# Tables of a state-space kernel laid out in groups of four columns

## The chip, the cores and the metric

One Trainium2 chip, one of its cores. The metric is the device time of one execution in microseconds (us); lower is better. A core has a matrix engine (PE, TensorE), a vector engine (DVE), a scalar engine (ACT), a general engine (POOL, GpSimd) and a queue engine (SP), each running its own instruction stream, held together by semaphores. Operands lie in SBUF, 128 partitions of some 200 KB; matmuls write to PSUM, 128 partitions with eight banks of 512 float32 values.

## What is computed

A layer of a state-space model with an MLP behind it, on a sequence of 2048 positions with 512 channels (all inputs bfloat16):

```python
def _A_ref(u, A_re, A_im, B_re, B_im, C_re, C_im, log_dt, Dskip):
    dt = jnp.exp(log_dt)[:, None]
    A = A_re + 1j * A_im; Bc = B_re + 1j * B_im; Cc = C_re + 1j * C_im
    logdA = dt * A
    dB = dt * Bc
    P = jnp.exp(logdA[:, :, None] * l[None, None, :])
    K = jnp.einsum("dn,dnl,dn->dl", Cc, P, dB).real
    # y = causal convolution of u with K (by FFT of length 4096), per channel
    return y + u * Dskip
def _B_ref(x, w1, b1, w2, b2):
    y = _layernorm(x)
    return _gelu(y @ w1 + b1) @ w2 + b2
h = x + _A_ref(_layernorm(x), ...)
return h + _B_ref(_layernorm(h), ...)
```

The part that matters here is K: for each of 512 channels d, a sum over n = 128 states of a complex exponential in the tap l. The kernel splits l into a coarse and a fine index, so that each channel's taps are a product of two small tables: 20 entries of the one kind (A) times 33 of the other (B), each with a real and an imaginary part.

## The kernel before

**Data.** All of SBUF is one arena `ar`; a view `V` is an offset, a type and a shape in it. The 512 channels are four blocks c = 0 to 3 of CW = 128 columns. For each block there are four tables, partition = state n: `EA[c]` and `IA[c]` (real and imaginary part, NA = 20 rows of 128 columns, bf16), `EB[c]` and `IB[c]` (NB = 33 rows). They are declared in L519 to L522, row by row: the element of row k and column d is at k*128 + d, so one column's entries are 256 bytes apart.

**How the tables are made.** The scalar engine writes magnitudes: `bexps` (L742 to L745) has 16 exponentials, each of which writes two rows (16 − e0 and 16 + e0) of all four blocks of EB, 1024 elements; `aexps` (L947 to L958) has 10, each for four rows of two blocks of EA. POOL sets the middle rows of EB and IB (L1360, L1361). Then come the angles. `chain` (L963 to L1011) does it for the B tables of two blocks at a time: matmuls (L979, L984) accumulate the angle in PSUM as an integer phase, the scalar engine takes 16 sines of 1024 elements (L992), and the vector engine multiplies magnitude by sine and cosine, the rows below the middle in reversed order and separately for real and imaginary part (L1004), the rows above in one instruction of 2048 elements for both (L1010). `chain1` (L1013 to L1035) does the same for the A table of one block: matmuls L1025 and L1028, 20 sines L1030, and 20 products L1034, each of which writes four rows of IA and EA by one instruction with two parts.

**How the taps are made.** `kgen` (L1042 to L1072), once for each block: for each of the 128 columns d two matmuls add into one PSUM area, L1058 with weights = column d of EA (128 x 20) and moving data = column d of EB (128 x 33), L1059 with IA and IB. Four column groups g of the array work at the same time, on columns 32g + i. Groups of 11, 11 and 10 values of i share a bank each (`KIS`); in a bank the sums lay as [k][i], k = 0 to 32: a matmul's 33 sums are n*4 bytes apart, n = 11 or 10. The work on the matrix engine comes in pieces of five or six i, and between the pieces the order puts other work. After it an eviction (L578 on the scalar, L580 on the vector engine) of 726 elements and one of 330 convert the sums to bf16 in `Kg` or `kgc`, whose innermost index is i; L1072 then adds the skip term.

**What stands around it.** `kspec` (L1074, matmuls L1088) and `kspec1` (L1100, matmuls L1113) take the taps to the spectrum; `lnorm` (L874, POOL's power at L649, L654, L882, L884) normalizes the input, `austage` (L897) and `fstage` (L918, L922) transform it; `inverse` (L1203, L1213) goes back, and the MLP (L1330, L1332, L1346, L1348) follows to the end.

**The order.** Nothing is scheduled on the chip. `S.add` records each operation with what it reads and writes; the list `ORDER` (L269 to L304) gives the order in which operations are written out, hence the order on each engine, and `SLOTS` the PSUM banks. An operation waits for an earlier one where the accesses of the two overlap.

Of the kernel before, what the change touches and what calls it, by code (L numbers as in the profile page):

```python
# [20 lines left out]
CW = 128  # L21
NCH = 4
# [221 lines left out]

class Two:
# [7 lines left out]
class VS(V):  # L253
# [57 lines left out]
class Sched:  # L311
    def __init__(self):
        self.ops = []
        self.wr, self.rd = {}, {}
        self.pr = 0.0

    def keys(self, x):
        if isinstance(x, V):
            return [(g, q) for q in range(x.p0 // 32, (x.p1 - 1) // 32 + 1) for g in range(x.lo // GK, (x.hi - 1) // GK + 1)]
        return (x,)  # L320

    def add(self, eng, cost, fn, r=(), w=(), new=(), lat=0.0, pr=None, byts=0, soft=(), softw=(), hv=None):
# [10 lines left out]
        for x in r:  # L333
            for k in self.keys(x):
                p = self.wr.get(k)
                if p is not None:
                    deps.add(p)
        for x in w:
            for k in self.keys(x):
# [67 lines left out]
def kernel(ctx, tc, A_u, A_A_re, A_A_im, A_B_re, A_B_im, A_C_re, A_C_im, A_log_dt, A_Dskip,  # L407
# [111 lines left out]
    EA = [at(EAo[c // 2] + c % 2 * ASZ, bf16, NA, CW) for c in range(NCH)]  # L519
    EB = [at(EB0 + c * BSZ, bf16, NB, CW) for c in range(NCH)]  # L520
    IA = [at(IAo[c // 2] + c % 2 * ASZ, bf16, NA, CW) for c in range(NCH)]
    IB = [at(IBo[c // 2] + c % 2 * BSZ, bf16, NB, CW) for c in range(NCH)]  # L522
# [219 lines left out]
    def bexps(pr):  # L742
        for e0 in range(1, 17):
            add("ACT", c_act(1024) + 0.03, lambda e, e0=e0: act.activation(multi(EB0, BSZ, bf16, NCH, NB, CW)[:, :, 16 - e0:17 + e0:2 * e0, :].rearrange("p c k d -> p k c d"), th.ap().rearrange("p k (c d) -> p k c d", c=NCH), ACT.Exp, scale=float(8 * e0)),  # L744
                r=[th, TBL], w=[EB[c][16 + z * e0] for z in (1, -1) for c in range(NCH)], pr=pr + 0.01 * e0)  # L745
# [183 lines left out]
    def ent(lo0, q, lo, n, rev=False):  # L929

        a = ar[:, lo0 // 2:lo0 // 2 + q].rearrange("p (c q) -> p c q", c=2)
        o = lo // 2
        a = a[:, :, o:o + n * CW].rearrange("p c (e d) -> p c e d", e=n)
        return a[:, :, ::-1, :] if rev else a

    def free(off, dims):

        a = ar[:, 0:1]
        return bass.AP(a.tensor, a.offset + off, [list(a.ap[0])] + dims)
# [4 lines left out]
    def regs(lo0, q, lo, n):  # L944
        return [at(lo0 + q * c + lo, bf16, n, CW) for c in range(2)]

    def aexps(hf, pr):  # L947
        for n in range(5):
            p = Ps()

            def fn(e, p=p, n=n):
                for j in range(4):
                    for g in range(4):
                        pe.matmul(pst(p)[32 * g:32 * g + 32, 256 * j:256 * j + 256], lhsT=W3[4 * n + j].ap(), rhs=S3[hf][g].ap(), start=True, stop=True, tile_position=(0, 32 * g))
            S.pr = pr + 0.01 * n
            add("PE", 0.45, fn, r=[W3, S3[hf]], w=[p], new=[p], soft=[TBL])
            add("ACT", c_act(1024), lambda e, p=p, n=n, hf=hf: act.activation(multi(EAo[hf] + 4 * n * 256, ASZ, bf16, 2, 4, CW).rearrange("p c a d -> p a c d"), pst(p).rearrange("p (a c d) -> p a c d", a=4, c=2), ACT.Exp),  # L957
                r=[p, TBL], w=[EA[2 * hf + c][4 * n + z] for c in range(2) for z in range(4)])  # L958
# [4 lines left out]
    def chain(hf, kind, pr):  # L963
# [4 lines left out]
        for gn, b0 in enumerate(groups):  # L968
# [3 lines left out]
            for cs in range(2):  # L972
# [19 lines left out]
                add("ACT", c_act(1024), lambda e, p=p, sc=sc, cs=cs: act.activation(sc[cs].ap().rearrange("p c e d -> p e c d"), pst(p, i16).rearrange("p (e c d two) -> p e c d two", e=4, c=2, two=2)[:, :, :, :, 0], ACT.Sin, scale=SINSC), r=[p, TBL], w=[sc[cs]])  # L992
            if kind == "B":
                todo = [((16 - b0 - 3) * 256, True), ((16 + b0) * 256, False)]
                e0, i0, q = EB0 + 2 * hf * BSZ, IBo[hf], BSZ
            else:
                todo = [(b0 * 256, False)]
                e0, i0, q = EAo[hf], IAo[hf], ASZ
            for n, (lo, rv) in enumerate(todo):
                rE, rI = regs(e0, q, lo, 4), regs(i0, q, lo, 4)  # L1000

                if rv:
                    for o0, m0, z in ((i0, rI, n), (e0, rE, 1 - n)):
                        add("DVE", c_dve(1024, 2), lambda e, lo=lo, sz=sc[z], e0=e0, o0=o0, q=q: dve.tensor_tensor(ent(o0, q, lo, 4, True), ent(e0, q, lo, 4, True), sz.ap(), ALU.mult), r=rE + [sc[z]], w=m0)  # L1004
                    continue

                def cfn(e, lo=lo, sc=sc, e0=e0, i0=i0, q=q, n=n):
                    z = sc.ap().rearrange("p z c e d -> p z c (e d)")
                    shp = [[q // 2, 2], [1, 4 * CW]]
                    dve.tensor_tensor(free((i0 + lo) // 2, [[(e0 - i0) // 2, 2]] + shp), free((e0 + lo) // 2, [[0, 2]] + shp), z[:, ::-1] if n else z, ALU.mult)  # L1010
                add("DVE", c_dve(2048, 2), cfn, r=rE + [sc], w=rE + rI)  # L1011

    def chain1(c, pr):  # L1013
        p = Ps("t", 2)
        for gn, b0 in enumerate((0, 4, 8, 12, 16)):
# [14 lines left out]
            add("ACT", c_act(1024), lambda e, sc=sc: act.activation(sc.ap().rearrange("p z a b -> p (z a b)"), pst(p, i16).rearrange("p (n two) -> p n two", two=2)[:, :, 0], ACT.Sin, scale=SINSC), r=[p, TBL], w=[sc])  # L1030
            rE, rI = EA[c][b0:b0 + 4], IA[c][b0:b0 + 4]

            def cfn(e, sc=sc, rE=rE, rI=rI):
                dve.tensor_tensor(free(rI.lo // 2, [[(rE.lo - rI.lo) // 2, 2], [1, 4 * CW]]), free(rE.lo // 2, [[0, 2], [1, 4 * CW]]), sc.ap().rearrange("p z a b -> p z (a b)"), ALU.mult)  # L1034
# [7 lines left out]
    def kgen(c, pr):  # L1042
# [3 lines left out]
        for grp in KIS:  # L1046
# [4 lines left out]
            for nb, (i0, n) in enumerate(grp):  # L1051
                for lo, hi in ((0, n // 2), (n // 2, n)):
                    def fn(e, p=p, nb=nb, i0=i0, n=n, lo=lo, hi=hi):
                        for i in range(lo, hi):
                            for g in range(4):
                                d = 32 * g + i0 + i
                                o = pst(p)[32 * g:32 * g + NA, 512 * nb:512 * nb + NB * n].rearrange("p (k i) -> p k i", i=n)[:, :, i]
                                pe.matmul(o, lhsT=Ar.ap()[:, :, d], rhs=Br.ap()[:, :, d], start=True, stop=False, tile_position=(0, 32 * g))  # L1058
                                pe.matmul(o, lhsT=Ai.ap()[:, :, d], rhs=Bi.ap()[:, :, d], start=False, stop=True, tile_position=(0, 32 * g))  # L1059
# [5 lines left out]
            def ofn(i0=i0, n=n, N=N):  # L1065
                a = ks()[:, :, i0:i0 + n * N]
                return a.rearrange("p k (b i) -> p b k i", b=N)

            def ifn(p=p, n=n, N=N):
                return pst(p).rearrange("p (b q) -> p b q", b=N)[:, :, 0:NB * n].rearrange("p b (k i) -> p b k i", i=n)  # L1070
# [288 lines left out]
    for c in range(NCH):  # L1359
        POOL(0.15, lambda c=c: gp.memset(EB[c][16].ap(), math.sqrt(0.5)), w=[EB[c][16]], pr=1.7)  # L1360
        POOL(0.15, lambda c=c: gp.memset(IB[c][16].ap(), math.sqrt(0.5)), w=[IB[c][16]], pr=1.71 + 0.01 * (c // 2))  # L1361
# [103 lines left out]
```

## Time and profile before

Device time in three runs: 236.57, 237.22 and 238.54 us, median 237.22.

| of the profiled execution | |
|---|---|
| time | 235.58 us |
| span of its instructions | 233.8 us |
| mean granted clock of the matrix engine | 0.967 |
| matrix engine (PE) busy | 204.2 us, 87% |
| vector engine (DVE) busy | 172.9 us, 74% |
| scalar engine (ACT) busy | 158.6 us, 68% |
| POOL busy | 13.4 us, 6% |
| kgen's matmuls | L1058 and L1059, 512 each |

Matmuls are pipelined, so their busy times overlap, and the distance between the starts of consecutive ones says what one costs on the engine. In rows of the timeline the first number is the start in us after the span's start, the second the length, "x4" the number of instructions put together in one row, and the bracket the idle time ahead of it and what ended it; "issue" there is time in which the engine waits for nothing that the profile shows. In rows of groups, the two numbers after the first bar are the busy time in us and the mean length of one in ns.

### The profile page before, as it was taken

The numbers are of one execution on the slowest core, as the hardware profiler recorded it, in microseconds if no ns is written. First come the engines' busy times: TensorE is split into PE (matmuls) and PEld (weight loads), VectorE is DVE, ScalarE is ACT, GpSimd is POOL, SyncE is SP. The second block draws the span as 40 slices with busy tenths as digits, with TensorE's granted clock in tenths as the row PEclk, the third lists the DMA queues.
The fourth block names the chain that finished last, engine by engine and source line by source line (L and its number), as shares of the span: only waits on it lengthen the run. The fifth ranks groups of instructions, "written<-read, shape, count | busy, mean of one in ns | idle before, by whom it ended". The sixth has DMA issues, their size and how long they took to land.

```text
span 233.8 us, 8092 instructions
## 1 busy us (share of the span) xinstructions
PE 204.2 (87%) x3608; PEld 117.0 (50%) x3616; DVE 172.9 (74%) x282; ACT 158.6 (68%) x194; POOL 13.4 (6%) x23
## 2 busy tenths in 40 slices
PE   7318878888998996999999968999999999999992
PEld 4305633335675455677567555654444344444551
DVE  2999999999979765659799999989955993010222
ACT  4999999999986893756898479685155308405500
POOL 3000300000160000000000010100000110000000
PEclk9965999999999998899999999999999999999998
DMA  5998263270000363346989966530333045002212
GB/s 157 185 172 138 62 185 95 60 254 13 6 6 3 98 159 138 99 105 195 221 141 230 311 159 161 137 90 12 81 77 91 5 100 126 20 0 59 56 40 61
DMA packets 43160, 25.18 MB, mean 108 GB/s; under 512 B 30195, under 2 KB 40693, under 8 KB 43126
## 3 DMA queue, kind: packets, MB, share of 16 engines
q1 hardware_dynamic: 42142, 23.67, 41.9%
q10 hardware_dynamic: 984, 1.00, 1.4%
q8 instruction: 28, 0.46, 0.8%
q14 instruction: 6, 0.05, 0.1%
HBM read 14.14 MB, written 5.28 MB: 83 GB/s over the span
## 4 chain that ended last, share of the span: by engine, by line
PE 51%; DVE 15%; DMA 11%; ACT 11%; issue 5%; SPq 3%; POOL 2%; DVEq 0%; ACTq 0%
PE ps L1330 16%; PE ps L1346 16%; DMA ar<-in_A_u_dram 5%; ACT ar L578 4%; PE ps L1213 4%; ACT ar L1030 3%; SPq L594 3%; ACT ar L992 3%; PE ps L1058 3%; DVE ar L874 3%; DVE ar L1203 2%; PE ps L918 2%; PE ps L1028 2%; PE ps L1059 2%; DVE ar L922 2%
## 5 line engine op out<-in xcount | busy, mean ns | idle before, releaser
L578 ACT CAST ar<-ps 128x1024 bf16<-128x1024 f32 (+4 forms) x64 | 56.8, 940 | 14.9 <-PE ps L1213 4.1
L1332 ACT ACTIVATE ar<-ps,ar 128x512 bf16<-128x512 f32 (+1 forms) x44 | 27.8, 685 | 36.3 <-PE ps L1330 25.7
L1330 PE MATMUL ps<-ar 128*128 128x512 bf16 (+1 forms) x176 | 41.1, 379 | 0.0
L1346 PE MATMUL ps<-ar 128*128 128x512 bf16 (+2 forms) x180 | 40.2, 366 | 0.7 <-DVE ar L1290 0.2
L1348 DVE TENSOR_TENSOR ar<-ps,ar 128x512 bf16<-128x512 f32 (+1 forms) x17 | 10.7, 656 | 31.8 <-PE ps L1346 25.1
L580 DVE CAST ar<-ps 128x1024 bf16<-128x1024 f32 (+3 forms) x22 | 21.5, 988 | 9.6 <-PE ps L1059 2.9
L1346 PEld LDWEIGHTS <-ar 128*128 128x128 bf16 (+1 forms) x187 | 18.0, 98 | 20.1 <-issue 1.2
L1330 PEld LDWEIGHTS <-ar 128*128 128x128 bf16 (+1 forms) x176 | 17.2, 100 | 20.1 <-DMA ar<-in_B_w_dram 0.2
L1203 DVE TENSOR_TENSOR ar<-ar 128x2048 bf16<-128x2048 bf16 x20 | 23.8, 1218 | 0.6 <-PE ps L1213 0.5
L1030 ACT ACTIVATE ar<-ps 128x1024 bf16<-128x1024 int16 x20 | 19.9, 1039 | 5.0 <-PE ps L1028 4.4
L1213 PE MATMUL ps<-ar 64*128 64x128 bf16 x672 | 21.4, 216 | 1.7 <-DVE ar L1203 1.2
L1213 PEld LDWEIGHTS <-ar 64*128 64x128 bf16 x672 | 18.8, 94 | 6.2 <-issue 2.9
L1058 PE MATMUL ps<-ar 128*20 128x33 bf16 x512 | 20.1, 249 | 0.7 <-issue 0.7
L1059 PE MATMUL ps<-ar 128*20 128x33 bf16 x512 | 20.0, 247 | 0.0
L1058 PEld LDWEIGHTS <-ar 128*20 128x20 bf16 x512 | 16.8, 124 | 4.5 <-issue 4.1
L649 POOL TENSOR_TENSOR ar<-ar 128x4 f32<-128x4 f32 (+1 forms) x6 | 10.3, 1716 | 137.2 <-DVE ar L654 129.9
L897 PE MATMUL ps<-ar 128*32 128x512 bf16 x256 | 16.5, 381 | 1.5 <-ACT ar L957 1.2
L1059 PEld LDWEIGHTS <-ar 128*20 128x20 bf16 x512 | 17.3, 127 | 0.8 <-issue 0.4
L1028 PE MATMUL ps<-ar 128*32 128x256 f16 (+2 forms) x288 | 13.4, 289 | 3.6 <-issue 1.8
L992 ACT ACTIVATE ar<-ps 128x1024 bf16<-128x1024 int16 x16 | 15.8, 1050 | 0.8 <-PE ps L984 0.7
L744 ACT ACTIVATE ar<-ar 128x1024 bf16<-128x1024 f32 x16 | 15.6, 1047 | 0.6 <-DVE ar L1247 0.6
L918 PE MATMUL ps<-ar 128*64 128x512 bf16 (+2 forms) x160 | 14.7, 303 | 0.3 <-ACT ar L578 0.2
(87 smaller groups left out, 258.9 us busy)
## 6 DMA issues: line engine op xcount, KB each, us to landing
ar<-in_A_u_dram SPq DMA_DIRECT2D x16, 128.0 KB, 6.2
out_dram<-ar SPq DMA_DIRECT2D x30, 64.0 KB, 2.0
ar<-in_A_u_dram SPq DMA_DIRECT2D x7, 256.0 KB
ar<-in_B_w_dram SPq DMA_DIRECT2D x2, 640.0 KB, 6.2
ar<-in_B_w_dram SPq DMA_DIRECT2D x3, 344.0 KB, 7.6
AK_d<-ar SPq DMA_DIRECT2D x2, 512.0 KB, 4.2
ar<-AK_d SPq DMA_DIRECT2D x2, 512.0 KB
AKc_d<-ar SPq DMA_DIRECT2D x4, 256.0 KB, 4.5
```

Source lines behind the costliest of these rows:

```text
L578: act.copy(out_fn(), in_fn())
L580: dve.tensor_copy(out_fn(), in_fn())
L918: pe.matmul(pst(p)[64 * h:64 * h + 64, w * (k + r):w * (k + r) + w], lhsT=T.ap()[:, f, r, :], rhs=v[f:f + 1].ap()[:, 0, :], start=True, st ...
L992: add("ACT", c_act(1024), lambda e, p=p, sc=sc, cs=cs: act.activation(sc[cs].ap().rearrange("p c e d -> p e c d"), pst(p, i16).rearrange(" ...
L1030: add("ACT", c_act(1024), lambda e, sc=sc: act.activation(sc.ap().rearrange("p z a b -> p (z a b)"), pst(p, i16).rearrange("p (n two) -> p ...
L1058: pe.matmul(o, lhsT=Ar.ap()[:, :, d], rhs=Br.ap()[:, :, d], start=True, stop=False, tile_position=(0, 32 * g))
L1059: pe.matmul(o, lhsT=Ai.ap()[:, :, d], rhs=Bi.ap()[:, :, d], start=False, stop=True, tile_position=(0, 32 * g))
L1203: dve.tensor_tensor(pq.ap().rearrange("p n d -> p (n d)"), a, b_, ALU.mult)
L1213: pe.matmul(pst(p)[:, 512 * h + 128 * k:512 * h + 128 * k + 128], lhsT=q.ap()[rows, x, :], rhs=TP[w].ap()[rows, f0 // 2 + k, :], start=(n ...
L1330: pe.matmul(pst(p)[:fs], lhsT=w1s[dc].ap()[:, fc * P:fc * P + fs], rhs=ybuf.ap().rearrange("p (t c) k -> p c t k", c=4)[:, dc], start=(dc ...
L1332: add("ACT", c_act(512, 1), lambda e, p=p, fc=fc, fs=fs: act.activation(hT.ap()[:fs, fc, :], pst(p)[:fs], ACT.Gelu_apprx_tanh, bias=b1_sb. ...
L1346: pe.matmul(pst(p)[:, c0:c1], lhsT=hT.ap()[:fs, fc, 128 * t:128 * t + 128], rhs=w2s[fc].ap()[:fs, c0:c1], start=(fc == 0), stop=(fc == NFC ...
```

## The change

The address of row k and column d in a table becomes (d // 4) * (4 * rows) + k * 4 + d mod 4, counted in bf16 elements: four neighbouring columns stand side by side, the rows of these four follow, then the next four columns. So the entries of one column are 8 bytes apart. Every instruction that writes or reads a table has its access pattern rewritten; the number of instructions and their sizes remain. The sums of one column lie side by side in PSUM ([i][k] instead of [k][i]), and the evictions turn them into the old order of `Kg` and `kgc` as they write. The tracking of what overlaps treats a table as a thing of its own (class `TV`, lists `tabs`, function `near`). In `ORDER` entry 272, a memset on POOL, stands later.

```diff
+class TV(V):
+    def __getitem__(self, i):
+        v = V.__getitem__(self, i)
+        return TV(v.ar, v.lo, v.dt, v.shape, v.p0, v.p1)
...
     def keys(self, x):
         if isinstance(x, V):
-            return [(g, q) for q in ... for g in range(x.lo // GK, (x.hi - 1) // GK + 1)]
+            far = 10 ** 6 * isinstance(x, TV)
+            return [(far + g, q) for q in ... for g in range(x.lo // GK, (x.hi - 1) // GK + 1)]
         return (x,)
+    def near(self, x):
+        if not isinstance(x, V):
+            return (x,)
+        far = 0 if isinstance(x, TV) else 10 ** 6
+        qs = range(x.p0 // 32, (x.p1 - 1) // 32 + 1)
+        return self.keys(x) + [(far + g, q) for lo, hi in self.tabs if x.lo < hi and lo < x.hi
+                               for q in qs for g in range(lo // GK, (hi - 1) // GK + 1)]
...
-    EA = [at(EAo[c // 2] + c % 2 * ASZ, bf16, NA, CW) for c in range(NCH)]
+    def tab(lo, n):
+        S.tabs.append((lo, lo + 2 * n * CW))
+        return TV(ar, lo, bf16, (n, CW))
+    EA = [tab(EAo[c // 2] + c % 2 * ASZ, NA) for c in range(NCH)]      # EB, IA, IB alike
+    def free(off, dims):
+        a = ar[:, 0:1]
+        return bass.AP(a.tensor, a.offset + off, [list(a.ap[0])] + dims)
...
# bexps: 16 exponentials of 1024
-act.activation(multi(EB0, BSZ, bf16, NCH, NB, CW)[:, :, 16 - e0:17 + e0:2 * e0, :].rearrange("p c k d -> p k c d"), ...
+act.activation(free(EB0 // 2 + 4 * (16 - e0), [[8 * e0, 2], [4 * NB, NCH * CW // 4], [1, 4]]), ...
# aexps
-act.activation(multi(EAo[hf] + 4 * n * 256, ASZ, bf16, 2, 4, CW).rearrange("p c a d -> p a c d"), ...
+act.activation(free(EAo[hf] // 2 + 16 * n, [[4 * NA, CW // 2], [4, 4], [1, 4]]), ...
# chain, rows above the middle (L1010); the reversed ones (L1004) have [[4 * NB, CW // 2], [-4, 4], [1, 4]]
-shp = [[q // 2, 2], [1, 4 * CW]]
+shp = [[4 * NB, CW // 2], [1, 16]]
 dve.tensor_tensor(free(io, [[eo - io, 2]] + shp), free(eo, [[0, 2]] + shp), ..., ALU.mult)
# chain1 (L1034)
-dve.tensor_tensor(free(rI.lo // 2, [[(rE.lo - rI.lo) // 2, 2], [1, 4 * CW]]), free(rE.lo // 2, [[0, 2], [1, 4 * CW]]), ...
+shp = [[4 * NA, CW // 4], [1, 16]]
+dve.tensor_tensor(free(io, [[eo - io, 2]] + shp), free(eo, [[0, 2]] + shp), ...
# kgen
-o = pst(p)[32 * g:32 * g + NA, 512 * nb:512 * nb + NB * n].rearrange("p (k i) -> p k i", i=n)[:, :, i]
-pe.matmul(o, lhsT=Ar.ap()[:, :, d], rhs=Br.ap()[:, :, d], start=True, stop=False, tile_position=(0, 32 * g))
-pe.matmul(o, lhsT=Ai.ap()[:, :, d], rhs=Bi.ap()[:, :, d], start=False, stop=True, tile_position=(0, 32 * g))
+o = pst(p)[32 * g:32 * g + NA, 512 * nb:512 * nb + NB * n].rearrange("p (i k) -> p i k", k=NB)[:, i, :]
+for ta, tb in ((Ar, Br), (Ai, Bi)):
+    pe.matmul(o, lhsT=free(ta.lo // 2 + d // 4 * 4 * NA + d % 4, [[4, NA]]),
+              rhs=free(tb.lo // 2 + d // 4 * 4 * NB + d % 4, [[4, NB]]), start=ta is Ar, stop=ta is Ai, ...)
...
-return a.rearrange("p k (b i) -> p b k i", b=N)
+return a.rearrange("p k (b i) -> p b i k", b=N)
...
-POOL(0.15, lambda c=c: gp.memset(EB[c][16].ap(), math.sqrt(0.5)), w=[EB[c][16]], pr=1.7)
+POOL(0.15, lambda c=c: gp.memset(free(EB[c].lo // 2 + 64, [[4 * NB, CW // 4], [1, 4]]), math.sqrt(0.5)), w=[EB[c][16]], pr=1.7)
```

The sines L992 and L1030 read PSUM and write their scratch in the order of the new tables (runs of four), so that the products read the scratch in one sweep.

More of the change, by code (lines that the diff above doesn't have):

```diff
@@ L333, in add @@
         for x in r:
-            for k in self.keys(x):
+            for k in self.near(x):
                 p = self.wr.get(k)
@@ L338, in add @@
         for x in w:
-            for k in self.keys(x):
+            for k in self.near(x):
                 p = self.wr.get(k)
@@ L991, in chain @@
                 first_ = o.i
[L992 to L998, printed above, removed]
```

55 lines of the change are left out of this document (27 added, 28 removed), and 4 rows, old and new, of the table ORDER.

## The prediction

> **What bounds the kernel now.** I read the page first, then the instructions in order of time on the matrix engine, and beside them those of the vector and scalar engines for the stretch from 57 to 108 us, where the stage that the change is about lies.
>
> ```profile
> span 233.8 us, 8092 instructions
> PE 204.2 (87%) x3608; PEld 117.0 (50%) x3616; DVE 172.9 (74%) x282; ACT 158.6 (68%) x194; POOL 13.4 (6%) x23
> PE 51%; DVE 15%; DMA 11%; ACT 11%; issue 5%; SPq 3%; POOL 2%; DVEq 0%; ACTq 0%
> ...
> L744 ACT ACTIVATE ar<-ar 128x1024 bf16<-128x1024 f32 x16 | 15.6, 1047 | 0.6 <-DVE ar L1247 0.6
> L1058 PE MATMUL ps<-ar 128*20 128x33 bf16 x512 | 20.1, 249 | 0.7 <-issue 0.7
> ```
>
> The profiled execution took 235.58 us: its span and 1.78 us around it; it lies 1.64 us under the median, 237.22, so I add 1.64 to what I work out in it. The kernel has no single bound: the chain of waits is half on the matrix engine. The change aims at kgen, 1024 matmuls of 33 columns. Their busy times (20.1 us for the half on L1058) overlap; what they cost on the engine is the distance of their starts.
>
> ```profile
> 57.98 0.27 PE L1058 MATMUL ps<-ar 128*20 128x33 bf16 x4
> ...
> 58.59 0.26 PE L1059 MATMUL ps<-ar 128*20 128x33 bf16 x4
> 58.79 0.41 PE L984 MATMUL ps<-ar 64*32 64x512 f16 x8
> ...
> 60.06 0.62 PE L918 MATMUL ps<-ar 128*64 128x512 bf16 x4
> ...
> 61.42 0.62 PE L984 MATMUL ps<-ar 64*32 64x512 f16 x16
> ...
> 63.03 0.35 PE L1028 MATMUL ps<-ar 128*32 128x128 f16 x12
> 63.20 0.40 PE L1025 MATMUL ps<-ar 65*32 65x512 f16 x4
> ...
> 65.03 0.27 PE L1058 MATMUL ps<-ar 128*20 128x33 bf16 x4 [0.26 <-issue]
> 65.07 0.28 PE L1059 MATMUL ps<-ar 128*20 128x33 bf16 x4
> ...
> 70.84 1.15 PE L897 MATMUL ps<-ar 128*32 128x512 bf16 x16 [0.28 <-DVE ar L882]
> 72.39 0.27 PE L1058 MATMUL ps<-ar 128*20 128x33 bf16 x4 [0.40 <-issue]
> ...
> 73.82 0.26 PE L1059 MATMUL ps<-ar 128*20 128x33 bf16 x4
> ...
> 75.01 1.91 PE L1088 MATMUL ps<-ar 20*128 20x512 bf16 x32
> ```
>
> Four matmuls, one for each group of 32 columns of the array, are one row here; I call them a quartet. Ten quartets stand from 57.98 to 58.59, nine distances of 0.068 us. All of kgen is 256 quartets: 17.4 us of the engine. Column by column (c = 0 to 3): c=0 and c=1 are done between 57.98 and 73.9, c=2 by 93.8, c=3 between 97.95 and 104.8. Where 12 matmuls of 128 columns read and write contiguous data (63.03 to 63.20), four take 0.057 us, though they have four times the columns.
>
> **Part 1: the matmuls' own pace.** Weights and moving columns go from 256 bytes apart to 8, the sums from up to 44 bytes apart to 4. The trace has no such matmul. The lower bound of the gain is none (0.068 stays). The upper one is the 0.04 at which two quartets follow each other after idle time (65.03, 65.07), when the first's weights are in place and only half of the old reading shows. The contiguous row at 0.057 with 128 columns says that a quartet of 33 needn't take 0.057, so I take 0.04: 0.028 saved per quartet, 7.2 us over all 256 if every one counted. Most don't, as the next parts show.
>
> [...]
>
> **Part 2: c=0 and c=1, with new waits.** Comparing the two programs, instruction order on each engine is unchanged (but for one memset on POOL), and no instruction is added. But the tables' rows now interleave, and the vector engine's product of L1034, which writes real and imaginary part in one instruction, is taken to touch the whole stretch that it spans. Three waits are new on the path: kgen's second quartet (58.04) waits for the L1034 product that runs second in the row at 58.24; the second part of c=0 (59.1) waits for the second product in the row at 60.70; and the product at 60.70 waits for the end of c=0's first part.
>
> ```profile
> 58.24 1.34 DVE L1034 TENSOR_TENSOR ar<-ar 128x1024 bf16<-128x1024 bf16 x2
> ...
> 60.70 1.28 DVE L1034 TENSOR_TENSOR ar<-ar 128x1024 bf16<-128x1024 bf16 x2
> ...
> 67.94 0.17 DVE L654 SCALAR_TENSOR_TENSOR ar<-ar 128x8 f32<-128x8 f32 x1 [1.43 <-POOL ar L649]
> ...
> 74.17 0.50 DVE L580 CAST ar<-ps 128x330 bf16<-128x330 f32 x1
> ...
> 101.70 1.23 DVE L580 CAST ar<-ps 128x1024 bf16<-128x1024 f32 x1 [2.28 <-PE ps L918]
> ```
>
> The products end at 58.24+1.34 = 59.58 and 60.70+1.28 = 61.98. Queued behind the waiting quartets on the matrix engine are L984 (58.79), L918 (60.06) and L984 (61.42), and for these the scalar engine waits. First: 59.65 + 9 x 0.04, then L984 at 60.1, 1.3 late. Second: 62.05 + 11 x 0.04 = 62.5, L918 2.4 late; then 0.55 of L918 and ten quartets, L984 at 63.6, 2.2 late.
>
> ```profile
> 59.27 1.97 ACT L992 ACTIVATE ar<-ps 128x1024 bf16<-128x1024 int16 x2 [0.41 <-PE ps L984]
> 61.12 1.02 ACT L578 CAST ar<-ps 128x1024 bf16<-128x1024 f32 x1
> 62.12 1.04 ACT L992 ACTIVATE ar<-ps 128x1024 bf16<-128x1024 int16 x1
> ...
> 68.50 0.88 ACT L884 ACTIVATE ar<-ar 128x512 bf16<-128x512 bf16 x1
> ...
> 73.47 0.77 ACT L578 CAST ar<-ps 128x726 bf16<-128x726 f32 x1 [0.40 <-PE ps L1059]
> ```
>
> The scalar engine is nearly full here: queued behind one another, two start 1.85 apart from 59.27, 0.925 each. From 62.12 on it runs 2.1 late. Seven instructions stand between there and 68.50, six of that size and one of 726 elements: 6.2 of the 6.38, and 0.08 of slack ahead of 62.12, so about 0.25 is made up. L884 ends at 69.38 + 1.85 = 71.2 instead of 69.38. The matmul L897 at 70.84 waits for it and, today, for the vector engine's L882, which itself hangs on POOL (67.94). So most of the delay falls into slack: L897 starts at about 71.35, 0.5 late. The quartets in between save their 0.028 each without effect. Behind L897, the last 22 quartets (72.39 to 73.89) take 0.88 instead of 1.50: 0.62 back; and of the 0.40 of idle "issue" I take half as gone. At L1088 (75.01) that makes 0.5 − 0.62 − 0.2 = −0.32, before the evictions.
>
> **Part 3: the evictions.** They now read PSUM contiguously and write single bf16 elements 64 or 128 bytes apart, where before they wrote 10 or 11 side by side.
>
> ```profile
> L578 ACT CAST ar<-ps 128x1024 bf16<-128x1024 f32 x47 | 46.3, 1036 | 11.7 <-PE ps L1213 4.1 <-PE ps L918 3.6 <-issue 1.6
> ...
> L578 ACT CAST ar<-ps 128x726 bf16<-128x726 f32 x4 | 3.1, 766 | 0.6 <-PE ps L1059 0.6
> ...
> L578 ACT CAST ar<-ps 128x330 bf16<-128x330 f32 x2 | 0.9, 441 | 0.0
> ```
>
> The rows give (1036 − 441)/694 = 0.86 ns per element, alike for all. No row writes single elements: the bounds are no cost and twice the time per element, 0.62 for 726 and 0.28 for 330. I take half, 0.3 and 0.15: no row prices it, and neither end is nearer. Two evictions of 726 (one ahead of L884, one at 73.47) and one of 330 (74.17) lie on the path to L1088: 0.75. So c=0 and c=1 end 0.43 later.
>
> [...]
>
> **Part 4: c=2 and c=3.**
>
> ```profile
> 92.13 0.40 PE L1028 MATMUL ps<-ar 128*32 128x256 f16 x4 [1.82 <-issue]
> 92.32 0.27 PE L1058 MATMUL ps<-ar 128*20 128x33 bf16 x4
> ...
> 93.75 0.25 PE L1059 MATMUL ps<-ar 128*20 128x33 bf16 x4
> ...
> 97.95 0.27 PE L1058 MATMUL ps<-ar 128*20 128x33 bf16 x4
> ...
> 101.04 0.63 PE L918 MATMUL ps<-ar 128*64 128x256 bf16 x8
> ...
> 104.79 0.62 PE L918 MATMUL ps<-ar 128*64 128x512 bf16 x4
> ```
> ```profile
> q8 instruction: 28, 0.46, 0.8%
> ```
>
> For c=2 the quartets before 92.13 end earlier, into a hole of 1.82 us in which the engine waits for nothing that the profile shows. I read it as instruction fetch: the instruction queue moves 0.46 MB in 28 pieces, 16 KB each, and a piece lies shortly before. A fetch that starts at its own time keeps the hole's end where it is; I count 0, with 0.6 as a bound. For c=3, 34 quartets lie between 97.95 and L918 at 101.04; 34 x 0.028 = 0.95, and the vector engine's eviction at 101.70, idle for 2.28 until that L918, starts the chain of work that follows. So 0.95 earlier; the bound above is 1.6, all quartets of c=3 up to 104.79.
>
> **Part 5: exponentials, sines, products, memsets.** The 16 exponentials of L744 write 8-byte runs, the 10 of L957 32-byte, the products 8- or 32-byte runs. No row writes 8-byte runs on the scalar engine. The bounds are no cost and 25%: where a single element may cost double, a run of four hops a quarter as often, 0.26 of L744's 1.05. I take none, since every form above has the same time per element whatever its runs. The POOL memset moves behind other POOL work; its reader starts after it either way.
>
> Sum: +0.43 + 0 − 0.95 = −0.5: 235.58 − 0.5 = 235.1, and with 1.64 the forecast is 236.7.
>
> **The rivals.**
>
> ```profile
> 88.40:91.90 3.50, 1.91 (x96) 1.60 (x88) 2.83 (x5) 1.06 (x1) 0.00 (x0) 1.00 0.40 163
> 91.90:95.30 3.40, 3.17 (x112) 2.27 (x112) 1.09 (x3) 2.02 (x3) 0.00 (x0) 0.50 0.02 5
> ```
>
> *Half clock.* (Rows: the stretch, the busy time of each engine, then the granted clock.) After a stretch with 1.91 of 3.5 us of the matrix engine busy, the next ran at granted clock 0.50. The new waits empty 58.05 to 59.65 and about 60.7 to 62.05; a stretch that takes in both would be as idle. Then L918 and L984, 0.55 each, take 1.1, and the scalar engine behind them is another 1.1 to 1.5 late, most of which reaches L1088, L884 having no slack left: +1.3, 238.0. For it: the windows' grid, continued back, has both holes nearly whole in one; against: where the grid falls may differ between executions, and the matrix engine has more to do than in the row. Chance 0.22.
>
> *The layout doesn't speed the matmuls.* The pace is set by weight loads and issue, not by the stride; for it, that the distance is 0.068 at 57.98 and also between 92.32 and 93.75 (22 quartets), at half the clock. Then the new waits stay, with no quartet made up: L918 at 62.05 + 11 x 0.068 = 62.8, the L984 behind it 2.65 late instead of 2.2, so L897 0.95 late; nothing comes back from the 22 quartets or in c=3; with 0.75 for the stores +1.7, 238.9. Chance 0.16; half of it, with stores at twice the time, above 239.6.
>
> *More comes through.* The stores cost nothing (−0.75), and the fetch hole of 1.82 moves or shrinks with the earlier quartets (about −1.2): 236.7 − 1.95, some 234.7, and 234.1 if the hole goes whole. Against it: a hole that a fixed fetch ends. Chance 0.18.
>
> *Slower: 8-byte runs on the scalar engine.* The exponentials of L744 take 25% more in the first 30 us. The engine idles 0.6 ahead of all of them together by the row above, so it is full there, and 16 x 0.26 = 4.2 arrives at the stage behind: 236.7 + 4.2 = 240.9. It ends over the old time once one costs 0.03 us more (16 x 0.03 = 0.5). For it: no row shows such a run. Against it: the equal time per element. Chance 0.12.
>
> **How the numbers follow.** The forecast has 0.32, with its own range 235.2 to 238.0. One per cent, about what a measurement can tell here, is 234.85 to 239.6. Faster: 0.18 of "more comes through" and 0.04 of the forecast's low end, 0.22. Slower: 0.12 for the exponentials, 0.08 of the unsped matmuls, 0.05 of the half clock with dear stores, 0.25. Within: 0.53. The range leaves out about a tenth on either side: 234.1 to 240.3.
>
> **What would show it.** Part 1: quartets 0.04 apart in kgen of c=3 (0.068 says no). Part 2: idle time of 1.6 and 1.3 us ahead of L1059 at 58 and 61, released by L1034; L897 near 71.35. Part 3: the 726-element eviction near 1.07 us. Part 4: the hole before 92 still there; L918 ahead of the first eviction of c=3 about 1 us earlier against L1113 of c=2. Part 5: L744 at 1047 ns, L1034 at 683. The clock in the windows after 57.8 tells of the first rival. The prediction is wrong if L744 or the sines grow, or if L1088 comes over 2 us later.

## The result, and the profile after

| | before | after |
|---|---|---|
| median of 4 runs | 237.55 us (236.57 to 238.54) | 251.56 us (250.32 to 252.0) |
| ratio, with its 95% interval | | 1.058 (1.052 to 1.064) |
| profiled execution: span, granted clock | 233.8 us, 0.967 | 249.6 us, 0.918 |

The changed kernel is 14 us slower. The page of its profile, in the same order as before:

```profile
span 249.6 us, 8101 instructions
## 1 busy us (share of the span) xinstructions
PE 205.5 (82%) x3608; PEld 114.0 (46%) x3616; DVE 175.5 (70%) x282; ACT 171.0 (68%) x194; POOL 12.0 (5%) x23
...
PEclk9957999999758799778579999999999999999999
...
PE 51%; ACT 18%; DVE 11%; DMA 8%; issue 7%; SPq 3%; DVEq 0%; ACTq 0%
```

The scalar engine's busy time went from 158.6 to 171.0 us, and its share of the chain of waits from 11 to 18%. The clock shows dips (7, 5, 8) in the middle that were not there. The groups by form, first of the scalar engine and then of the vector engine, say where the time went:

```profile
L770 ACT ACTIVATE ar<-ar 128x1024 bf16<-128x1024 f32 x16 | 15.6, 1046 | 0.6 <-DVE ar L1258 0.6
L604 ACT CAST ar<-ps 128x726 bf16<-128x726 f32 x4 | 13.6, 3396 | 0.0
...
L604 ACT CAST ar<-ps 128x330 bf16<-128x330 f32 x2 | 3.6, 1799 | 0.0
```
```profile
L1045 DVE TENSOR_TENSOR ar<-ar 128x1024 bf16<-128x1024 bf16 x20 | 13.2, 682 | 2.1 <-ACT ar L1040 1.7
...
L606 DVE CAST ar<-ps 128x330 bf16<-128x330 f32 x2 | 3.2, 1616 | 2.5 <-PE ps L1070 2.5
```

Line numbers have moved: L604 and L606 are the evictions (L578, L580 before), L770 the exponentials, L1045 the products, L1070 both of kgen's matmuls, L995, L944, L923 and L1099 the earlier L984, L918, L897 and L1088, L1083 the earlier L1072. The evictions of kgen's sums take 3396 ns instead of 766, and 1799 and 1616 instead of 441 and 502. That is 4 x 2.63 + 2 x 1.36 = 13.2 us of added work on the scalar engine and 2 x 1.11 = 2.2 on the vector engine; neighbouring instructions overlap a little (its groups by form add up to 165.3 us before and 179.7 after, its busy times are 158.6 and 171.0), so the busy time of the scalar engine rose by less. The exponentials (1046 ns, 1047 before) and the products (682, 683) cost the same. The matrix engine in order of time:

```profile
58.37 0.19 PE L1070 MATMUL ps<-ar 128*20 128x33 bf16 x1
60.14 0.56 PE L1070 MATMUL ps<-ar 128*20 128x33 bf16 x39 [1.57 <-DVE ar L1045]
60.63 0.41 PE L995 MATMUL ps<-ar 64*32 64x512 f16 x8
...
62.53 0.60 PE L1070 MATMUL ps<-ar 128*20 128x33 bf16 x47 [1.36 <-DVE ar L1045]
63.06 1.06 PE L944 MATMUL ps<-ar 128*64 128x512 bf16 x4
...
75.58 1.35 PE L923 MATMUL ps<-ar 128*32 128x512 bf16 x16
...
82.08 2.68 PE L1099 MATMUL ps<-ar 20*128 20x512 bf16 x32 [2.47 <-DVE ar L1083]
...
105.38 0.62 PE L1124 MATMUL ps<-ar 20*128 20x256 bf16 x16 [1.54 <-DVE ar L1083]
...
118.58 1.04 PE L1124 MATMUL ps<-ar 20*128 20x256 bf16 x16 [3.27 <-DVE ar L1083]
```

Against before, L923 comes 4.7 us later (75.58 against 70.84), L1099 7.1 later (82.08 against 75.01), and the span ends 15.8 later. The last three rows, with idle time released by L1083, are each the first use of new taps: L1083 needs their last eviction, and it is the scalar engine's that it waits for. The vector engine ahead of L1099:

```profile
78.99 1.63 DVE L606 CAST ar<-ps 128x330 bf16<-128x330 f32 x1
...
81.85 0.18 DVE L1083 TENSOR_TENSOR ar<-ar 128x32 bf16<-128x32 bf16 x1 [1.23 <-ACT ar L604]
```

The scalar engine at these places:

```profile
66.57 3.42 ACT L604 CAST ar<-ps 128x726 bf16<-128x726 f32 x1
...
75.97 6.70 ACT L604 CAST ar<-ps 128x330 bf16<-128x330 f32 x4
...
101.80 3.32 ACT L604 CAST ar<-ps 128x726 bf16<-128x726 f32 x1
...
112.63 5.70 ACT L604 CAST ar<-ps 128x1024 bf16<-128x1024 f32 x3 [1.14 <-PE ps L944]
```

A row with several instructions names the form of its first; the row at 75.97 and the one at 112.63 each have an eviction of 726 and one of 330 among them. All four evictions of 726 elements are on the path: the first ahead of L923, the others ahead of L1099 and of the two L1124. The last part of the loss lies where nothing of the change runs. These are windows (the stretch, then the busy time of each engine, the granted clock, the DMA share), the changed kernel first, then the kernel before at the place that answers to it:

```profile
117.20:127.40 10.20, 8.82 (x132) 5.67 (x131) 5.71 (x8) 6.15 (x7) 0.00 (x0) 0.50 0.51 125
```
```profile
105.40:115.60 10.20, 9.84 (x268) 6.24 (x268) 8.60 (x12) 7.65 (x10) 0.00 (x0) 1.00 0.84 203
```

The matrix engine sits idle for 3.27 us ahead of 118.58, and 10.2 us from 117.2 on are at half the clock. In them, the first 1.4 us still idle, it gets through 132 matmuls where 268 were done before.

### The profile page after: what moved, and what is told of

It is laid out like the page before. It is cut to its first block, busy times and chain, and to the rows that moved or that the text cites. A ratio compares the mean times of both kernels' runs of the same rounds, so it can differ in the third digit from the quotient of the medians.

```text
span 249.6 us, 8101 instructions
## 1 busy us (share of the span) xinstructions
PE 205.5 (82%) x3608; PEld 114.0 (46%) x3616; DVE 175.5 (70%) x282; ACT 171.0 (68%) x194; POOL 12.0 (5%) x23
## 4 chain that ended last, share of the span: by engine, by line
PE 51%; ACT 18%; DVE 11%; DMA 8%; issue 7%; SPq 3%; DVEq 0%; ACTq 0%
PE ps L1341 15%; PE ps L1357 15%; ACT ar L604 9%; ACT ar L1040 5%; PE ps L1224 4%; DMA ar<-in_A_u_dram 4%; PE ps L944 4%; SPq L620 3%; ACT ar L1003 3%; PE ps L923 2%; PE ps L1038 2%; DVE ar L1214 2%; DVE ar L900 2%; PE ps L1124 2%; DMA ar<-S_d 2%
## 5 line engine op out<-in xcount | busy, mean ns | idle before, releaser
L604 ACT CAST ar<-ps 128x1024 bf16<-128x1024 f32 (+4 forms) x64 | 69.2, 1156 | 17.7 <-PE ps L944 5.5
L1343 ACT ACTIVATE ar<-ps,ar 128x512 bf16<-128x512 f32 (+1 forms) x44 | 27.8, 685 | 36.3 <-PE ps L1341 25.7
L606 DVE CAST ar<-ps 128x1024 bf16<-128x1024 f32 (+3 forms) x22 | 23.7, 1089 | 13.0 <-PE ps L1124 3.7
L1224 PE MATMUL ps<-ar 64*128 64x128 bf16 x672 | 22.2, 221 | 1.8 <-DVE ar L1214 1.2
L923 PE MATMUL ps<-ar 128*32 128x512 bf16 x256 | 17.9, 409 | 1.3 <-ACT ar L968 1.2
L1070 PE MATMUL ps<-ar 128*20 128x33 bf16 x1024 | 12.9, 201 | 6.4 <-DVE ar L1045 2.9
L1070 PEld LDWEIGHTS <-ar 128*20 128x20 bf16 x1024 | 11.3, 101 | 12.7 <-issue 10.3
L944 PE MATMUL ps<-ar 128*64 128x512 bf16 (+2 forms) x160 | 16.7, 341 | 0.4 <-ACT ar L604 0.2
L770 ACT ACTIVATE ar<-ar 128x1024 bf16<-128x1024 f32 x16 | 15.6, 1046 | 0.6 <-DVE ar L1258 0.6
L675 POOL TENSOR_TENSOR ar<-ar 128x4 f32<-128x4 f32 (+1 forms) x6 | 8.5, 1423 | 143.8 <-DVE ar L680 136.4
L1045 DVE TENSOR_TENSOR ar<-ar 128x1024 bf16<-128x1024 bf16 x20 | 13.2, 682 | 2.1 <-ACT ar L1040 1.7
L948 DVE TENSOR_TENSOR ar<-ps,ar 128x512 bf16<-128x512 f32 x16 | 10.4, 684 | 3.0 <-PE ps L944 3.0
```

Of the source, the lines that this page charges most:

```text
L604: act.copy(out_fn(), in_fn())
L606: dve.tensor_copy(out_fn(), in_fn())
L923: pe.matmul(pst(p)[32 * j:32 * j + 32, 512 * z:512 * z + 512], lhsT=BX.ap()[:, f0 + z, 16 - 16 * c:48 - 16 * c], rhs=src[2 * j + c].ap(), ...
L944: pe.matmul(pst(p)[64 * h:64 * h + 64, w * (k + r):w * (k + r) + w], lhsT=T.ap()[:, f, r, :], rhs=v[f:f + 1].ap()[:, 0, :], start=True, st ...
L1070: pe.matmul(o, lhsT=free(ta.lo // 2 + d // 4 * 4 * NA + d % 4, [[4, NA]]), rhs=free(tb.lo // 2 + d // 4 * 4 * NB + d % 4, [[4, NB]]), star ...
L1224: pe.matmul(pst(p)[:, 512 * h + 128 * k:512 * h + 128 * k + 128], lhsT=q.ap()[rows, x, :], rhs=TP[w].ap()[rows, f0 // 2 + k, :], start=(n ...
```

## The experiments

Two theories were set against each other at first: that the single-element stores carry nearly all of the loss (S), or that the new waits and the half clock behind them carry a large part (W).

**Run stores.** The changed kernel, with nothing altered but the order in which the evictions go through the data:

```diff
-return a.rearrange("p k (b i) -> p b i k", b=N)
+return a.rearrange("p k (b i) -> p b k i", b=N)
...
-return pst(p)...[:, :, 0:NB * n].rearrange("p b (i k) -> p b i k", k=NB)
+return pst(p)...[:, :, 0:NB * n].rearrange("p b (i k) -> p b k i", k=NB)
```

> The changed kernel, but its evictions of kgen's sums go through the data with the channel innermost: they write runs of 11 or 10 bf16 elements, as before the change, and read PSUM 132 bytes apart at every element. Tables, order of the sums in PSUM and all new waits stay. Theory S (the loss is the single-element stores, 2.63 us more for each eviction of 726 elements and 1.1 to 1.36 for each of 330): those evictions are back at about 0.77 and 0.44 to 0.50 us, kgen's four matmuls stay 0.036 us apart, and the time is 236 to 239 us. Rival W (the new waits at 58 to 62 us, and the half clock that the idle matrix engine brings, carry a large part): over 242 us. Rival H (reading PSUM with hops costs as much as the hopping stores did): the 726-element eviction stays over 2 us and the time over 246 us.

Measured: 238.61 us, ratio to before 1.011 (1.004 to 1.019). In the groups of the scalar engine:

```profile
L604 ACT CAST ar<-ps 128x726 bf16<-128x726 f32 x4 | 3.1, 764 | 3.1 <-PE ps L1070 3.1
```

The eviction is back at 764 ns although it now reads PSUM in hops of 132 bytes, so rival H falls. The two lines of order are worth 12.95 us by the medians, 4.7 of the 5.8 per cent by the ratios. All new waits are still there, so taken by themselves they hold at most the 1.1% that is left.

**Single stores in the old kernel.** The reverse edit in the kernel before:

```diff
-return a.rearrange("p k (b i) -> p b k i", b=N)
+return a.rearrange("p k (b i) -> p b i k", b=N)
...
-return pst(p)...[:, :, 0:NB * n].rearrange("p b (k i) -> p b k i", i=n)
+return pst(p)...[:, :, 0:NB * n].rearrange("p b (k i) -> p b i k", i=n)
```

> The kernel before, with its tables, waits and PSUM order, but its evictions go through the data with the tap index innermost: they write single elements 128 or 64 bytes apart, and read PSUM 44 or 40 bytes apart. Theory S: the 726-element eviction is near 3.4 us, the 330-element one near 1.7, and the kernel takes 249 to 254 us, somewhat above the changed one since its matmuls are not faster. Rival W: under 243 us.

Measured: 249.44 us (2 runs), ratio 1.055 (1.045 to 1.065), with

```profile
L578 ACT CAST ar<-ps 128x726 bf16<-128x726 f32 x4 | 13.5, 3383 | 0.0
```

The stores alone, without the new tables and without a new wait, cost the old kernel 12.9 us. S holds from both sides. The price includes what comes behind the evictions: between 56 and 130 us this trace has 20.5 us at half the clock, where the kernel before has 3.4.

**The price by itself.** Twenty copies of 704 elements from PSUM, behind the last store of the kernel before: ten forms on the scalar engine (L1438 to L1447), the same ten on the vector engine (L1448 to L1457).

```diff
+act.copy(free(q0, [[1, 704]]), flat)                      # L1438 contiguous; L1439 runs of 11, L1440 of 8, L1441 of 4
+act.copy(free(q0, [[32, 352], [1, 2]]), ...)              # L1442 pairs every 64 bytes
+act.copy(free(q0, [[1, 22], [32, 32]]), ...)              # L1443 single elements every 64 bytes
+act.copy(free(q0, [[8, 704]]), flat)                      # L1444 single elements every 16 bytes
+act.copy(free(q0, [[2, 704]]), flat)                      # L1445 single elements every 4 bytes
+act.copy(ar[...].bitcast(f32)..., ...)                    # L1446 single float32 every 88 bytes
+act.copy(free(q0, [[22, 32], [1, 22]]), hop)              # L1447 runs, with hops of 132 bytes in PSUM
```

> The kernel before, with 20 copies of 704 elements from PSUM to a free place behind its last store, ten on the scalar and then the same ten on the vector engine: bf16 contiguous; runs of 11, 8, 4 and 2 elements every 64 bytes; single elements every 64, 16 and 4 bytes; single float32 elements every 88 bytes; contiguous bf16 with hops of 132 bytes in PSUM. Theory S, with the price in the hops of the store: contiguous, runs of 4 or more and hopping reads take 0.7 to 0.8 us on the scalar engine, single elements near 3.3 us. If it is the write of a part of a 4-byte word that costs, pairs and single float32 are cheap and all single bf16 dear, those 4 bytes apart too; if it is the step from line to line, those 4 bytes apart are cheap and single float32 dear. The kernel's own part of the time doesn't change; the probe adds about 30 to 40 us behind it.

The scalar engine's groups:

```profile
L1444 ACT CAST ar<-ps 128x704 bf16<-128x704 f32 x1 | 3.3, 3268 | 0.0
L1443 ACT CAST ar<-ps 128x704 bf16<-128x704 f32 x1 | 3.2, 3209 | 0.0
L1446 ACT COPY ar<-ps 128x704 f32<-128x704 f32 x1 | 1.8, 1772 | 0.0
L1445 ACT CAST ar<-ps 128x704 bf16<-128x704 f32 x1 | 0.9, 939 | 0.0
...
L1442 ACT CAST ar<-ps 128x704 bf16<-128x704 f32 x1 | 0.7, 747 | 0.0
L1438 ACT CAST ar<-ps 128x704 bf16<-128x704 f32 x1 | 0.7, 746 | 7.4 <-PE ps L1346 7.4
...
L1447 ACT CAST ar<-ps 128x704 bf16<-128x704 f32 x1 | 0.7, 746 | 0.0
```

Pairs, longer runs and hopping reads cost nothing over a contiguous copy. A single bf16 costs 3209/704 = 4.56 ns, a single float32 1772/704 = 2.5 ns. Neither of the two simple rules that were expected holds alone: single bf16 4 bytes apart are nearly free (939), so it isn't the part of a word as such, and 4-byte stores pay for hopping too, but half as much. The probe made the kernel 264.05 us long, 27.8 over the 236.3 us of the kernel before it, somewhat less than the 30 to 40 expected.

**Which stride set the matmuls' pace.** Four kernels take the layout apart: PSUM order alone, both tables without the PSUM order, the A tables alone, the B tables alone.

```diff
# before_psum_contiguous: the kernel before, and
+o = pst(p)[...].rearrange("p (i k) -> p i k", k=NB)[:, i, :]
# tables_only: the changed kernel, and
+o = pst(p)[...].rearrange("p (k i) -> p k i", i=n)[:, :, i]
# weights_only
+pe.matmul(o, lhsT=free(ta.lo // 2 + d // 4 * 4 * NA + d % 4, [[4, NA]]), rhs=tb.ap()[:, :, d], ...)
# moving_only
+pe.matmul(o, lhsT=ta.ap()[:, :, d], rhs=free(tb.lo // 2 + d // 4 * 4 * NB + d % 4, [[4, NB]]), ...)
```

> The kernel before with its tables (256 bytes apart) and no new waits; only the sums of a column lie side by side in PSUM, and the evictions write runs of 11 or 10. If PSUM's stride set the matmuls' pace: four matmuls 0.036 to 0.045 us apart and 235 to 237 us. If the tables' stride set it: 0.066 to 0.069 as before, and 237 to 238.5 us.

> The changed kernel's tables and waits, but the sums in PSUM and the evictions as before the change (a matmul's sums 44 or 40 bytes apart). If the tables' stride set the matmuls' pace: four matmuls 0.036 to 0.045 us apart and 236 to 239 us. If PSUM's stride set it: 0.066 to 0.069, and with the new waits unrepaid 238 to 241 us.

> Only the A tables (the matmuls' weights, 20 entries) have the new layout; the B tables (moving data, 33 entries) lie as before the change, 256 bytes apart. Sums side by side in PSUM, evictions with run stores. The new waits of kgen are not there, since it was the reads of the B tables that were taken to overlap with the products. If the weights' stride set the pace: four matmuls 0.036 to 0.045 us apart, and 234.5 to 236.5 us by theory W, 236 to 238 by theory F. If the moving data's stride set it: 0.060 to 0.069 apart and the time of the kernel before.

> The opposite: only the B tables have the new layout, the A tables lie as before the change; run stores; the new waits stay. If the moving data's stride set the pace: four matmuls 0.036 to 0.045 us apart. If the weights' did: 0.060 to 0.069, and about 238 to 240 us.

Rows of the timelines, in the same order (two rows of the first kernel, one of each other):

```profile
58.40 0.27 PE L1058 MATMUL ps<-ar 128*20 128x33 bf16 x4
...
59.02 0.26 PE L1059 MATMUL ps<-ar 128*20 128x33 bf16 x4
```
```profile
66.14 0.63 PE L1070 MATMUL ps<-ar 128*20 128x33 bf16 x48
```
```profile
58.00 0.79 PE L1081 MATMUL ps<-ar 128*20 128x33 bf16 x40
```
```profile
60.07 0.59 PE L1069 MATMUL ps<-ar 128*20 128x33 bf16 x39 [1.66 <-DVE ar L1044]
```

With PSUM order alone ten quartets span nine distances of 0.069 us: no change, and 236.87 us, 1.000 of before (0.997 to 1.004). For the rows with 48, 40 and 39 matmuls the starts in the trace give quartets 0.036, 0.057 and 0.042 us apart in these stretches. So the pace came from the tables' stride, mostly the moving side's, and PSUM's stride had no part in it at full clock; that weights alone would do it or not at all was expected, and they did a small part. At half clock PSUM's stride did show, in the one trace that has new tables and strided sums:

```profile
62.94 0.85 PE L1070 MATMUL ps<-ar 128*20 128x33 bf16 x47 [1.37 <-DVE ar L1045]
```

Here quartets are 0.053 us apart, at a granted clock of 0.50; the changed kernel, with its sums side by side, has 0.036 at that clock. The times: both tables 239.12 us, 1.012 (1.005 to 1.019), just over the 236 to 239 expected; weights alone 236.18, 1.001 (0.997 to 1.006); moving alone 239.26 in one run. Kernels with the new B tables, hence with the new waits, are 1% slower than before (one of the two by a single run); those without are level with it. None is faster.

**What is left: waits or fetch?** Once the stores are cheap, matmuls at 0.036 should gain something, and don't. The trace of the version with run stores shows this (three rows of four in which the engine waits for nothing that the profile shows):

```profile
75.55 0.96 PE L1070 MATMUL ps<-ar 128*20 128x33 bf16 x86 [1.46 <-issue]
...
95.59 0.40 PE L1038 MATMUL ps<-ar 128*32 128x256 f16 x4 [3.01 <-issue]
...
108.42 0.78 PE L1070 MATMUL ps<-ar 128*20 128x33 bf16 x64 [2.29 <-issue]
```

With one of 0.54 at 103.60 that is 7.3 us between 56 and 125, against 2.8 before (0.26, 0.40, 1.82 and one of 0.35). Each of the three ends 2.4 us after a transfer of 16 KB began on the instruction queue (at 73.1, 93.2 and 106.0 us in the trace). The hole ahead of c=2's last quartets ends 2.1 to 2.5 us after such a start in ten other traces too, that of the kernel before among them (89.9 and 92.13). The 7.3 us are the largest such sum, from the longest execution of the four (240.88 us). Other traces with a pace of 0.036 to 0.042 have 4.7 us (both tables) and 4.5 (moving side alone), and the changed kernel, which its evictions hold up, 2.7; those with a pace of 0.057 to 0.069 have 2.3 to 3.8. So the rise is there, but smaller than this one trace says. Theory F: the matmuls now run ahead of their instructions. Three kernels on this and the waits. The first splits each product so that no wait arises:

```diff
-dve.tensor_tensor(free(io, [[eo - io, 2]] + shp), free(eo, [[0, 2]] + shp), z, ALU.mult)
+dve.tensor_tensor(free(io, shp), free(eo, shp), z[:, 0], ALU.mult)
+dve.tensor_tensor(free(eo, shp), free(eo, shp), z[:, 1], ALU.mult)
```

> The kernel with the changed tables and run stores, with each product of the A chains (L1045) written as two instructions of 512 elements, one for each table, instead of one of 1024 with two parts. No part of kgen then waits for a product of the next block. Theory W (what is left over the old time comes from those waits and the half clock after them): no idle time ahead of kgen at 58 and 61 us, 2 to 3 us less than with the waits, 235 to 236.5 us, in spite of some 0.1 us more of the vector engine for each of 20 products. Theory F (kgen's matmuls now run faster than their instructions can be fetched, and this caps the gain): the idle time put down to issue in kgen stays at 5 to 8 us (2.5 before the change), and the time is 236 to 238 us, no better than the kernel before.

Measured: 238.26 us, 1.010 (1.004 to 1.016). The two waits are gone (0.72 us of idle time is left ahead of kgen, at 58.63), but a product now takes two instructions of 0.42 us, 0.84 instead of 0.68, and the vector engine became the late one:

```profile
72.38 1.15 PE L923 MATMUL ps<-ar 128*32 128x512 bf16 x16 [1.82 <-DVE ar L908]
...
94.58 0.29 PE L1038 MATMUL ps<-ar 128*32 128x256 f16 x4 [2.70 <-issue]
```

W's 235 to 236.5 us failed, but the remedy has a price of its own, so this doesn't decide. F's 5 to 8 us of issue time failed as well: it is 4.4. The second leaves the products whole and moves kgen's first three pieces in `ORDER` behind L995, L944 and L995 (and exchanges the two PSUM slots concerned):

```diff
 ORDER:
-626, 658, 510, 382, 388, 512, 660, 502, 746, 662, 748, 524, 514, 516,
+626, 510, 382, 388, 512, 502, 746, 748, 524, 514, 658, 660, 662, 516,
```

> The kernel with the changed tables and run stores; in the order, the first three pieces of kgen for c=0 (22 and 11 pairs of columns' matmuls) stand behind the three pieces of other work on the matrix engine (L995, L944, L995) that they stood ahead of. The waits for the products are still there, but nothing that another engine waits for is queued behind them. Theory W (the waits cost through what is queued behind): L923 of the second half starts near 71 us as before the change instead of 73, and the time is 234.5 to 236.5 us, 2 us or more under the version with run stores alone. Theory F (fetch caps the gain): L923 near 71 too, but 4 to 7 us of idle time put down to issue in kgen, against 2.5 before the change, and a time of 235.5 to 237.5 us.

The control with the same order in the kernel before:

> The control: the kernel before the change with only this order. There are no new waits, and the matmuls are 0.068 us apart, so moving the pieces delays kgen by 1 to 1.5 us within a stretch where it has slack: 236 to 238 us, no gain by either theory.

Measured: 238.57 us, 1.006 (1.002 to 1.010), and for the control 238.0 us, 1.006 (1.002 to 1.009). Both theories had given less, 236.5 and 237.5 us at most. L920 (the earlier L897) stands at 72.17, between the 71 expected and the 73.0 of the version with run stores. The order costs the old kernel as much as this one is behind: if that price is the same in both, which no run shows, the changed tables without blocking waits are level with the kernel before. But then the gain of the faster matmuls is missing, as F has it. The largest of its holes, 5.9 us in all:

```profile
74.96 0.97 PE L1067 MATMUL ps<-ar 128*20 128x33 bf16 x87 [1.74 <-issue]
...
93.61 0.40 PE L1035 MATMUL ps<-ar 128*32 128x256 f16 x4 [1.62 <-issue]
...
105.07 0.78 PE L1067 MATMUL ps<-ar 128*20 128x33 bf16 x64 [1.20 <-issue]
```

The third takes half of kgen's instructions away from that kernel; it leaves out the products of the imaginary tables, so its taps are not the layer's:

```diff
-for ta, tb in ((Ar, Br), (Ai, Bi)):
+for ta, tb in ((Ar, Br),):
```

> The kernel with kgen later, without the second matmul of each pair: the products of the imaginary tables are left out of the sums, so kgen issues 1024 instructions less on the matrix engine (512 matmuls and their weight loads) and 2 x 2048 bytes per 32 columns less have to be fetched. Theory F: the idle time put down to issue between 56 and 125 us falls from 4 to 7 us to under 3, and the time is 3 us or more under the same kernel with both matmuls. Theory W alone: the issue time stays, and the time falls by no more than 1.5 us.

One run: 235.83 us, 2.7 under the median of the ten runs with both matmuls, which lie between 236.73 and 239.72. Between 56 and 125 us no row has idle time put down to issue any more; what L920 now waits for is the vector engine:

```profile
71.13 1.90 PE L920 MATMUL ps<-ar 128*32 128x512 bf16 x16 [2.35 <-DVE ar L905]
```

F's sign is there, its 3 us were not quite reached; this run also went through 17 us of half clock from 66.8 on, but the holes near 93 and 105 us, at full clock, are gone too. The instruction queue has fewer pieces, 24 where it had 28:

```profile
q8 instruction: 24, 0.39, 0.7%
```

The 1024 instructions left out were four pieces of 16 KB, so one holds 256, of 64 bytes each. In none of the thirteen traces do two pieces start less than 3.25 us apart. From these figures the stream brings at most some 79 instructions per us for long (an estimate, 256 / 3.25), where four matmuls and four weight loads in 0.036 us ask for 222, and in 0.069 us for 116. So the issue time goes with the instructions that kgen issues; one run shows it, and it drops their work on the engine with them. That the 16 KB transfers are what is waited for is read off their times only.

## Why the prediction was wrong

**Part 3 failed, and with it the time.** It said of the evictions: "No row writes single elements: the bounds are no cost and twice the time per element, 0.62 for 726 and 0.28 for 330. I take half, 0.3 and 0.15". They measured 2.63, and 1.36 and 1.11. The upper bound was a multiple picked without a row, and it was short by a factor of four; the value taken was short by nine. The mechanism and the places of the large ones were named: one eviction ahead of L884, one ahead of L1088. With the measured sizes in the same sum, c=0 and c=1 end −0.32 + 2 x 2.63 + 1.11 = 6.05 later; the trace has 7.1. The 330 of the vector engine, which the sum has on the path, wasn't on it: it ended at 80.62, 1.2 us ahead of L1083. It was the scalar engine's 330, at 75.97, that stood ahead of the last 726; with its 1.36 the sum is 6.3. For c=2 and c=3 the prediction left the evictions out of the sum altogether, and there the path lost another 5.2: 2.7 from L1088 to the first L1113, 2.4 from there to the second.

The probe has the price on the vector engine as well: a single bf16 every 64 bytes took 4.56 ns (3207 for 704), a single float32 every 88 bytes 2.51 (1768). By the first, 330 elements come to an estimated 1.5 us, near the 1.62 that the eviction took; it grew by 1.11, where the prediction has 0.15.

**Part 1 was right.** 0.04 was forecast for a quartet; it is 0.036. The reason given for 0.04 is not shown: of the four weight loads of the quartet at 65.03, one stood ahead of the idle time (64.52) and three ran at 65.03. That PSUM's order had no share in it at full clock was not forecast.

**Part 2 was right in its waits.** 1.6 and 1.3 us of idle time were forecast, released by L1034's successor; 1.57 and 1.36 are in the trace, and L995 stands at 60.63, L944 at 63.06 (60.1 and 62.5 forecast, in a run that reached kgen 0.4 later). L897 near 71.35 was missed by 4.2: the first eviction's 2.63, the 0.4 at the start, and a rest that lies beside the half clock (0.50 from 69.4 to 76.3) and is not split further.

**The first rival happened too.** The window from 62.6 to 66.0 ran at 0.50, and L944's 1.06 us instead of 0.62 shows it; in the 3.4 us ahead of it the matrix engine was busy for 1.10. The four other traces in which these waits show have a stretch at 0.50 that starts between 60.8 and 62.6 as well, and none without them has one between 56 and 66. The 238.0 given for this rival lies near the 238.61 that the run stores leave, partly by luck: it has 0.75 for the stores and −0.95 for c=3 in it, neither of which is in that run, and the two nearly cancel. Five more stretches at 0.50 followed, from 69.4, 83.1, 100.1, 107.0 and 117.2; in the 3.4 us ahead of each the matrix engine was busy for 1.24, 1.02, 1.03, 1.72 and 1.51 us. Ahead of the third lies the hole of part 4, ahead of the others waits for the evictions. All six starts are whole multiples of 3.4 us apart, like the windows of the rival. The last stretch, 10.2 us, carries the loss from 12.2 us (118.58 against 106.35) to 15.8 at the end of the span.

**Part 4** kept the hole of c=2 in place: 1.82 before, 2.14 at 100.36 after. Its gain for c=3 came in the changed kernel and went nowhere. Its first matmuls and the L944 behind its last, in the changed kernel and then with run stores:

```profile
108.45 0.90 PE L1070 MATMUL ps<-ar 128*20 128x33 bf16 x80
...
113.69 0.62 PE L944 MATMUL ps<-ar 128*64 128x512 bf16 x4
```
```profile
101.17 0.54 PE L1070 MATMUL ps<-ar 128*20 128x33 bf16 x40
...
109.13 1.06 PE L944 MATMUL ps<-ar 128*64 128x512 bf16 x4
```

The stretch takes 5.24 us in the changed kernel, against 6.84 before (97.95 to 104.79): 1.6 less, the prediction's bound. The evictions behind it cost more than that. With run stores it takes 7.96, with 2.83 us of issue in it: there the holes eat the gain. "More comes through" had the hole shrink with earlier quartets; it grew.

**Part 5 was right**, as the two groups show, and the slower rival (8-byte runs on the scalar engine) is false: 1046 ns against 1047 for the exponentials. No rival held single-element stores at more than twice the time, so the range, 234.1 to 240.3, left out the size that decided.

What stays open: how the 1.1% that the run-store version is slower divides among waits, half clock and fetch. Each remedy tried brought a price of its own, and of the versions tried none beats the kernel before.

## What to carry to other kernels

A layout change that makes one side contiguous can move the hops to the other side: price the side that gets them by a probe of that very store before anything else, since the nearest row can be several times off (here 0.86 ns per element against 4.56). A cost that no row shows has no upper bound from a round factor. And a matmul that is made faster may pay only while its instructions arrive (here 222 per us asked for, and an estimated 79 brought); this case points to it without settling it, so count instructions per microsecond as one of the bounds.

## What the runs showed of the hardware

- A bf16 store that hops by 64 or by 16 bytes at every element takes 4.6 ns on the scalar and on the vector engine alike (3209 and 3207 ns for 704 every 64 bytes, 3268 and 3266 every 16), a 4-byte one that hops by 88 bytes 2.5 ns (1772 and 1768); pairs of bf16 every 64 bytes are free (747 against 746 ns contiguous on the scalar engine, 892 and 892 on the vector engine), and reads of PSUM that hop by 132 bytes too (746 and 892).
- Matmuls of 33 columns with 20 weights: 0.069 us for four with table entries 256 bytes apart, 0.036 with 8 bytes; the moving side alone brings it to 0.042, the weights alone to 0.057. The stride of their sums in PSUM (4 or 44 bytes) made no difference at full clock; at a granted clock of 0.50 strided sums gave 0.053 where sums side by side gave 0.036.
- With 95 to 111 of these matmuls and as many weight loads per microsecond (0.042 to 0.036 us for four), idle time without any wait between 56 and 125 us rose from 2.8 us to between 4.4 and 7.3 in the five traces with cheap stores, and vanished in one run with half the instructions. The pieces of 256 instructions never started less than 3.25 us apart.
